# Decode step on one core: V caches issued from ScalarE's DMA queue instead of SyncE's

## The chip, the cores and the metric

The kernel runs on one core of one Trainium2 chip. Its time is the device time of one execution in microseconds (us); 121.77 us is the median of three runs before the change (121.72 to 121.81). A profile is one further execution, in which the hardware profiler records every instruction and every DMA packet. Its times are counted from the first instruction. In the views PE is TensorE (matmuls), PEld its weight loads, DVE VectorE, ACT ScalarE, POOL GpSimd; SPq and ACTq are the instructions with which SyncE and ScalarE issue DMA transfers. MiB below is 1,048,576 bytes; the profile's GB/s are in 10^9 bytes.

## The reference

One decode step for 8 sequences (one token each), model width 512. The input is normalised; one branch is attention over the last 1024 positions of a cached K and V (32 query heads, 8 key/value heads, head size 128), the other a gated feed-forward network (width 1792); the output is `x + attention * silu(ffn)`.

```python
xn = layernorm(x)                                  # x: 8 x 1 x 512
q  = (xn @ wq).reshape(8, 1, 32, 128)              # wq: 512 x 4096
k, v = k_cache[:, :, 3072:], v_cache[:, :, 3072:]  # 8 x 8 x 1024 x 128 each, 4 query heads share one
p  = softmax(q k^T / sqrt(128));  o = p v
s  = o.reshape(8, 1, 4096) @ wo                    # wo: 4096 x 512
f  = (gelu(xn @ w_gate) * (xn @ w_up)) @ w_down    # 512 x 1792, 512 x 1792, 1792 x 512
return x + s * silu(f)
```

Everything is bf16 in memory. What has to be read: K and V of a sequence 2 MiB each (8 sequences, together 32 MiB), wq 4 MiB, w_gate, w_up and w_down 1.75 MiB each, wo 4 MiB.

## The kernel before, in words

All large tensors go through one ring of 8 buffers of 2 MiB (`slot`). A buffer is given to the next tile as soon as the program's order says that its former tile is done with. A sequence's K or V (`load_cache`, L72) is two transfers of 1 MiB, `g` = 0 and 1, 128 rows of 8192 bytes each; called k3a and k3b below for sequence 3. wq is two transfers of 2 MiB (L93, rows of 16384 bytes); gate, up and down are one transfer each with rows of 14336 bytes (L422, L425); wo is three transfers of 1 MiB with rows of 8192 bytes and three last pieces of 640, 256 and 128 KiB (L436). All of these are issued by SyncE, in this order:

k0, wq, k1, v0, k2, v1, k3, v2, k4, v3, k5, v4, k6, v5, k7, v6, v7, gate, up, down, wo.

Only x (8 KiB) is issued by ScalarE, in one transfer. In the built program the completion of each transfer is counted on one of eight semaphores, taken by turns in the program's order, and a transfer is issued only when the transfer eight places before it in that order has landed. So at most eight transfers are under way, and each engine's queue issues in its own order: a transfer that must wait (for the eighth before it, or for its ring buffer) holds up those behind it on the same engine, and on ScalarE the arithmetic behind it too.

The work per sequence b, in the order of the loop at the kernel's middle: VectorE turns k(b+1)a (`turn_k`, L234), takes the row maximum of the scores of b (L305 to L312), turns k(b+1)b, and turns the probabilities (`turn_p`, L328). ScalarE makes the bias (L315), the exp (L317), and copies the result out of PSUM (`keep_o`, L352). TensorE does the scores of b+1 (L295) in two halves, the gathering of b-1's heads between them (L360, L364), and then the product with V (`values`, L339), whose second half of 32 matmuls reads the b half of V. The exp of b+1 stands behind `keep_o(b)` on ScalarE, and `keep_o(b)` needs `values(b)`, which needs V of b. `turn_k(b+1, 0)` stands ahead of the maximum of b on VectorE.

After the loop, strictly one behind the other: `gather(7)`, `regroup(1)` (L375 to L391), the gate and up products (L450), the gelu on ScalarE and VectorE (L460 to L473), the down product (L479), the product with wo (L498, `s_ps`, four groups of 32 matmuls), two VectorE operations (L506, L508) and the store. TensorE takes its instructions in that order, so the feed-forward products come after `values(7)` although they need nothing of it.

Of the kernel before, what the change touches and what calls it, by code (L numbers as in the profile page):

```python
# [21 lines left out]
def kernel(  # L22
# [13 lines left out]
    nc = tc.nc  # L36

    B, Sq, D = A_x.shape
# [23 lines left out]
    def slot(name):  # L62
        return ring.tile([P, 2 * ROW], BF16, name=name, tag="slot")


    x_sb = keep.tile([B, D], BF16, name="x_sb")
    nc.scalar.dma_start(out=x_sb, in_=A_x.flatten_outer_dims())

    def load_cache(cache, b, name):
        t = slot(name).rearrange("p (g x) -> p g x", g=NG)  # L70
        for g in range(NG):
            nc.sync.dma_start(  # L72
                out=t[:, g],
                in_=cache[b, g * HG : (g + 1) * HG, win0:Sk, :].rearrange(
                    "n (p c) d -> p n (c d)", c=C
                ),
            )
        return t

    k_sb, v_sb = {}, {}  # L80

    def load_k(b):
        k_sb[b] = load_cache(A_k_cache, b, "k_sb")

    def load_v(b):
        v_sb[b] = load_cache(A_v_cache, b, "v_sb")

    load_k(0)
    wq_v = A_wq.rearrange("(p k) n -> p k n", k=NK)
    wq_sb = []  # L90
    for i in range(2):
        t = slot("wq_sb").rearrange("p (k n) -> p k n", k=NK // 2)
        nc.sync.dma_start(out=t, in_=wq_v[:, i * (NK // 2) : (i + 1) * (NK // 2), :])  # L93
        wq_sb += [t[:, k, :] for k in range(NK // 2)]
    load_k(1)
    load_v(0)


# [3 lines left out]
        out=ident,  # L102
        in_=ident,
# [13 lines left out]
        out=xpad,  # L117
        in_=xpad,
# [17 lines left out]
        out=xhat,  # L136
# [9 lines left out]
    with tc.tile_pool(name="ps_x", bufs=1, space=PSUM) as ps_x:  # L146
# [26 lines left out]
        out=hv,  # L173
        in_=hv,
# [7 lines left out]
        out=neg_st,  # L182
        in_=neg_st,
# [8 lines left out]
        out=neg_mv,  # L192
        in_=neg_mv,
# [12 lines left out]
    for g in range(NG):  # L206
        nc.vector.tensor_reduce(
            out=sel[:, g, g * qd : (g + 1) * qd],
            in_=ident.rearrange("p (t g h) -> p g h t", t=4, g=NG)[:, g],
# [5 lines left out]
        out=own, in_=ident.rearrange("p (i e) -> p e i", e=8), axis=AX.X, op=ALU.add  # L215
    )
    pick = consts.tile([P, 4 * NU], BF16, name="pick")
    with nc.allow_low_precision(reason="sums of zeros and a single one"):
        nc.vector.tensor_reduce(
            out=pick, in_=ident.rearrange("p (a e) -> p a e", e=8), axis=AX.X, op=ALU.add  # L220
# [11 lines left out]
    def turn_k(b, g):  # L232
        t = kT_pool.tile([P, ROW], BF16, name="kT")
        nc.vector.transpose(out=t.bitcast(I32), in_=k_sb[b][:, g].bitcast(I32))  # L234
        kT[b, g] = t
# [7 lines left out]
    with tc.tile_pool(name="ps_q", bufs=1, space=PSUM) as ps_q:  # L243
# [10 lines left out]
        for half in range(2):  # L254
# [3 lines left out]
            for i in range(4 * half, 4 * half + 4, 2):  # L258
                sl = slice(i * 512, (i + 2) * 512)
                nc.vector.transpose(out=q_t[:, sl].bitcast(I32), in_=q_bf[:, sl].bitcast(I32))  # L260

    q_v = q_t.rearrange("p (g h m b r w) -> p m b r w g h", g=NG, h=qd, m=2, b=B, r=RB)
    for j in range(4):
        sl = slice(32 * j, 32 * j + 32)
# [15 lines left out]
    def scores(b, g):  # L280
        if g == 0:
            S[b] = ps_s.tile([P, 2, 512], FP32, name="S_ps")
            for half in range(2):
                nc.tensor.matmul(  # L284
                    S[b][:, half, :],
                    neg_st.rearrange("p j h -> p (j h)"),
                    neg_mv.rearrange("p a n -> p (a n)"),
                    start=True,
                    stop=False,
                )  # L290
        kv = kT[b, g].rearrange("p (c m i w) -> p c m i w", m=2, i=32, w=2)
        for m in range(2):
            for w in range(2):
                for half in range(2):
                    nc.tensor.matmul(  # L295
                        S[b][:, half, :],
                        qbd[:, m, b, w, g, :],
                        kv[:, half * 16 : (half + 1) * 16, m, :, w],
                        start=False,
                        stop=(g == NG - 1 and m == 1 and w == 1),  # L300
                    )

    def softmax(b):
        mx = two.tile([P, 1], FP32, name="mx")
        nc.vector.tensor_reduce(  # L305
            out=mx, in_=S[b].rearrange("p a c -> p (a c)"), axis=AX.X, op=ALU.max
        )

        m2 = two.tile([64, 1], FP32, name="m2")
        nc.vector.tensor_tensor(out=m2, in0=mx[0:64, :], in1=mx[64:128, :], op=ALU.max)  # L310
        m1 = two.tile([32, 1], FP32, name="m1")
        nc.vector.tensor_tensor(out=m1, in0=m2[0:32, :], in1=m2[32:64, :], op=ALU.max)  # L312
        nb = two.tile([P, 1], FP32, name="nb")
        for j in range(4):
            nc.scalar.mul(nb[32 * j : 32 * j + 32, :], m1, -inv)  # L315
        P_sb[b] = two.tile([P, C // 2, 32, 2], BF16, name="P_sb")
        nc.scalar.activation(  # L317
            out=P_sb[b].rearrange("p c i w -> p c w i"),
            in_=S[b].rearrange("p a (c w i) -> p (a c) w i", w=2, i=32),
            func=ACT.Exp,  # L320
            bias=nb,
            scale=inv,
            accum_out=sums[:, b : b + 1],
        )

    def turn_p(b):
        pT[b] = two.tile([P, C // 2, Hq, 2], BF16, name="pT")
        nc.vector.transpose(  # L328
            out=pT[b].rearrange("p c h w -> p (c h w)").bitcast(I32),
            in_=P_sb[b].rearrange("p c i w -> p (c i w)").bitcast(I32),  # L330
        )

    def values(b):
        O_ps[b] = ps_o.tile([P, NG, Dh], FP32, name="O_ps")
        for g in range(NG):
            vv = v_sb[b][:, g].rearrange("p (c d) -> p c d", d=Dh)
            for c in range(C):
                t = c % 4
                nc.tensor.matmul(  # L339
                    O_ps[b][32 * t : 32 * t + 32, g, :],  # L340
                    pT[b][:, c // 2, :, c % 2],
                    vv[:, c, :],
                    start=(c < 4),
                    stop=(c >= C - 4),
                )
# [4 lines left out]
    def keep_o(b):  # L350
        O_sb[b] = two.tile([P, NG, Dh], FP32, name="O_sb")
        nc.scalar.copy(out=O_sb[b], in_=O_ps[b])  # L352

    def gather(b):
        q = b % 4
        if q == 0:
            o_ps[b // 4] = ps_g.tile([P, Dh + 1], FP32, name="o_ps")
        o = o_ps[b // 4][32 * q : 32 * q + 32, :]
        for g in range(NG):
            nc.tensor.matmul(  # L360
                o[:, 0:Dh], sel[:, g, :], O_sb[b][:, g, :], start=(g == 0), stop=(g == NG - 1)
            )
        for g in range(NG):
            nc.tensor.matmul(  # L364
                o[:, Dh : Dh + 1],
                sel[:, g, :],
                sums[:, b : b + 1],
                start=(g == 0),
                stop=(g == NG - 1),
            )  # L370

    def regroup(q):

        rc = two.tile([P, 1], FP32, name="rc")
        nc.vector.reciprocal(out=rc, in_=o_ps[q][:, Dh : Dh + 1])  # L375
        o_x = two.tile([P, 8, Dh], BF16, name="o_x")
        nc.vector.scalar_tensor_tensor(
            out=o_x,
            in0=o_ps[q][:, 0:Dh].unsqueeze(1).broadcast_to([P, 8, Dh]),
            scalar=rc,  # L380
            in1=own.unsqueeze(2).broadcast_to([P, 8, Dh]),
            op0=ALU.mult,
            op1=ALU.mult,
        )
        ox_v = o_x.rearrange("p h (e j) -> p j (h e)", j=8)
        r_ps = ps_g.tile([P, 8, 4, NU], FP32, name="r_ps")
        for j in range(8):
            nc.tensor.matmul(
                r_ps[:, j], ox_v[:, j], pick, start=True, stop=True
            )  # L390
        nc.vector.tensor_copy(  # L391
            out=oT[:, :, :, 4 * RB * q : 4 * RB * (q + 1) : RB],
            in_=r_ps.rearrange("p j b u -> p j u b"),
        )
# [3 lines left out]
    for b in range(B):  # L398
        if b + 2 < B:
            load_k(b + 2)  # L400
        if b + 1 < B:
            load_v(b + 1)
            turn_k(b + 1, 0)
        softmax(b)
        if b + 1 < B:
            scores(b + 1, 0)
        if b >= 1:
            gather(b - 1)
        if b + 1 < B:
            turn_k(b + 1, 1)  # L410
            scores(b + 1, 1)
        turn_p(b)
        values(b)
        keep_o(b)
        if b == 4:
            regroup(0)
# [29 lines left out]
    for n, ws in (("z_ps", wgu[0]), ("u_ps", wgu[1])):  # L446
# [15 lines left out]
        out=z2, in0=z2, scalar1=0.044715, scalar2=1.0, op0=ALU.mult, op1=ALU.add  # L462
# [11 lines left out]
        out=hT.rearrange("p j b -> p (j b)"), in_=h_bf.rearrange("p (y j) -> p j y", j=NJ)  # L474
    )
    f_ps = ps_f.tile([P, DT], FP32, name="f_ps")
    for j in range(NJ):
# [11 lines left out]
        out=g_sb, in0=g_sb, scalar1=0.5, scalar2=0.5, op0=ALU.mult, op1=ALU.add  # L489
# [5 lines left out]
    for u in range(NU):  # L495
# [15 lines left out]
        out=out_f.rearrange("b (t d) -> t b d", t=4), in_=out_sb[0 : P : RB, :]  # L511
# [31 lines left out]
```

## Time and profile before

| what | before |
|---|---|
| median of three runs | 121.77 us |
| the profiled execution's own time | 121.8 us |
| its span, first to last instruction | 119.7 us |
| time outside the span | 2.1 us |
| busy: PE, DVE, ACT | 74.1, 75.8, 31.4 us |
| moved by DMA | 47.61 MB, mean 398 GB/s over the span |
| share of the SyncE queue's packets in 16 engines' span | 94.5% |
| granted TensorE clock, mean over the span | 0.837 |
| issue to landing of a K or V transfer, median | 19.9 and 19.6 us |

The profile page gives each engine's busy time, a strip of 40 slices with the busy share in tenths, the DMA queues by bytes, the chain of work that ended last, and groups of like instructions with their mean time and the idle time before them. The DMA share is the mean busy share of 16 DMA engines; near 1.0 none of them has an idle moment. Queue q1 carries SyncE's transfers, q10 ScalarE's, q8 and q14 fetch instructions.

### The profile page before, as it was taken

To read this page: it belongs to the slowest core of one execution; us is meant where nothing else is said; L and a number is where in the kernel's file an instruction comes from. 1 tells how busy PE (TensorE), PEld (TensorE's weight loads), DVE (VectorE), ACT (ScalarE), POOL (GpSimd) and SP (SyncE) were. 2 spreads that over 40 slices of the span, in tenths; PEclk is the share of its full clock that TensorE was granted. 3 is DMA by queue.
4 is the path that set the end of the run, shared out by engine and by line. 5 is a ranking of instruction groups with operands and counts; after the bars stand their busy time and mean duration, and the time that the engine had idled before them with its cause. 6 is when DMAs were issued, how large, how long until landed. Compare 5 with 4: busy or idle time off the path is not lost.

```text
span 119.7 us, 2300 instructions
## 1 busy us (share of the span) xinstructions
PE 74.1 (62%) x992; PEld 38.7 (32%) x992; DVE 75.8 (63%) x101; ACT 31.4 (26%) x75; POOL 3.2 (3%) x10
## 2 busy tenths in 40 slices
PE   0100499811994988969687684992994547535460
PEld 0100133300341544535443351450353433134340
DVE  3698820499739999999859959909943232651010
ACT  4600000676007151441612510700616110200000
POOL 2150000000000000000000000000000000000000
PEclk9999999985599999999999998599589755555555
DMA  2999999999999999999999999999999999999930
GB/s 66 394 457 433 411 416 427 430 433 422 427 427 433 419 419 427 435 411 430 430 433 405 430 430 430 411 430 435 424 419 447 422 451 412 434 403 430 402 118 3
DMA packets 6254, 47.61 MB, mean 398 GB/s; under 512 B 732, under 2 KB 868, under 8 KB 1124
## 3 DMA queue, kind: packets, MB, share of 16 engines
q1 hardware_dynamic: 6228, 47.46, 94.5%
q8 instruction: 8, 0.13, 0.4%
q10 hardware_dynamic: 16, 0.01, 0.0%
q14 instruction: 2, 0.02, 0.0%
HBM read 47.46 MB, written 0.01 MB: 397 GB/s over the span
## 4 chain that ended last, share of the span: by engine, by line
DMA 63%; PE 16%; DVE 14%; issue 2%; ACT 2%; SPq 1%; DVEq 0%
DMA wo_sb<-in_A_wo_dram 20%; DMA k_sb<-in_A_k_cache_dram 17%; DMA v_sb<-in_A_v_cache_dram 16%; DMA wq_sb<-in_A_wq_dram 9%; PE q_ps L247 8%; PE S_ps L295 6%; DVE kT L234 5%; DVE qbd L269 2%; DVE mx L305 2%; DVE q_both L260 1%; ACT P_sb L317 1%; PE s_ps L498 1%; DVE q_both L257 1%; SPq L72 1%; PE O_ps L339 1%
## 5 line engine op out<-in xcount | busy, mean ns | idle before, releaser
L295 PE MATMUL S_ps<-kT,qbd 128*128 128x512 bf16 x128 | 34.4, 416 | 14.9 <-DVE kT L234 11.5
L234 DVE STREAM_TRANSPOSE kT<-k_sb 128x2048 int32<-128x2048 int32 x16 | 36.5, 2289 | 4.6 <-DMA k_sb<-in_A_k_cache_dram 4.6
L295 PEld LDWEIGHTS <-qbd 128*128 128x128 bf16 x128 | 12.9, 103 | 32.4 <-issue 17.0
L247 PE MATMUL q_ps<-wq_sb,xnR 128*128 128x512 bf16 x32 | 9.8, 482 | 8.8 <-DMA wq_sb<-in_A_wq_dram 8.8
L315 ACT ACTIVATE nb<-m 32x1 f32<-32x1 f32 x32 | 6.4, 201 | 22.7 <-DVE m L312 22.4
L305 DVE TENSOR_REDUCE mx<-S_ps 128x1 f32<-128x1024 f32 x8 | 9.6, 1195 | 4.1 <-PE S_ps L295 4.1
L317 ACT ACTIVATE P_sb<-S_ps,nb 128x1024 bf16<-128x1024 f32 x8 | 11.1, 1391 | 0.3
L339 PE MATMUL O_ps<-v_sb,pT 128*32 128x128 bf16 x512 | 9.3, 228 | 2.6 <-DVE pT L328 2.6
L339 PEld LDWEIGHTS <-pT 128*32 128x32 bf16 x512 | 7.8, 101 | 5.6 <-issue 3.0
L352 ACT COPY O_sb<-O_ps 128x256 f32<-128x256 f32 x8 | 3.0, 372 | 23.5 <-PE O_ps L339 23.5
L247 PEld LDWEIGHTS <-xnR 128*128 128x128 bf16 x32 | 3.7, 118 | 14.6 <-issue 12.6
L328 DVE STREAM_TRANSPOSE pT<-P_sb 128x512 int32<-128x512 int32 x8 | 5.7, 711 | 3.4 <-ACT P_sb L317 2.8
L257 ACT CAST q_both<-q_ps 128x512 bf16<-128x512 f32 x6 | 3.0, 613 | 16.7 <-PE q_ps L247 16.7
L360 PE MATMUL o_ps<-O_sb,sel 128*32 128x128 f32 x32 | 6.1, 325 | 0.9 <-ACT O_sb L352 0.9
L498 PE MATMUL s_ps<-wo_sb,oT 128*32 128x128 bf16 x128 | 4.4, 307 | 3.4 <-DMA wo_sb<-in_A_wo_dram 3.3
L284 PE MATMUL S_ps<-neg_mv,neg_st 128*128 128x512 bf16 x16 | 4.8, 381 | 1.9 <-DVE q_both L257 1.9
L257 DVE CAST q_both<-q_ps 128x512 bf16<-128x512 f32 x2 | 1.3, 672 | 6.9 <-ACT q_both L257 6.9
L360 PEld LDWEIGHTS o_ps<-O_sb,sel 128*32 128x32 f32 x32 | 3.4, 128 | 5.0 <-issue 1.7
L498 PEld LDWEIGHTS <-oT 128*32 128x32 bf16 x128 | 3.5, 136 | 4.4 <-issue 4.2
L506 DVE TENSOR_TENSOR y<-s_ps,g_sb 128x128 f32<-128x128 f32 x1 | 0.3, 290 | 6.9 <-PE s_ps L498 6.9
L239 DVE MEMSET qbd<- 128x4096 uint32 x1 | 3.5, 3472 | 0.8 <-issue 0.8
L479 PE MATMUL f_ps<-wd_sb,hT 128*32 128x128 bf16 x56 | 1.7, 311 | 3.2 <-DVE hT L473 3.2
(64 smaller groups left out, 48.9 us busy)
## 6 DMA issues: line engine op xcount, KB each, us to landing
k_sb<-in_A_k_cache_dram SPq DMA_DIRECT2D x16, 1024.0 KB, 19.9
v_sb<-in_A_v_cache_dram SPq DMA_DIRECT2D x16, 1024.0 KB, 19.6
wq_sb<-in_A_wq_dram SPq DMA_DIRECT2D x2, 2048.0 KB, 11.3
wo_sb<-in_A_wo_dram SPq DMA_DIRECT2D x3, 1024.0 KB, 25.0
wgu_sb<-in_B_w_gate_dram SPq DMA_DIRECT2D x1, 1792.0 KB, 21.3
wgu_sb<-in_B_w_up_dram SPq DMA_DIRECT2D x1, 1792.0 KB
wd_sb<-in_B_w_down_dram SPq DMA_DIRECT2D x1, 1792.0 KB, 24.9
wo_sb<-in_A_wo_dram SPq DMA_DIRECT2D x1, 640.0 KB, 24.1
```

The lines of the kernel that those rows point to most:

```text
L234: nc.vector.transpose(out=t.bitcast(I32), in_=k_sb[b][:, g].bitcast(I32))
L247: nc.tensor.matmul(q_ps[i], xnR[:, k, :, :].rearrange("p j b -> p (j b)"), wq_sb[k][:, i * 512 : (i + 1) * 512], start=(k == 0), stop=(k = ...
L257: e(out=q_bf[:, i * 512 : (i + 1) * 512], in_=q_ps[i])
L284: nc.tensor.matmul(S[b][:, half, :], neg_st.rearrange("p j h -> p (j h)"), neg_mv.rearrange("p a n -> p (a n)"), start=True, stop=False,)
L295: nc.tensor.matmul(S[b][:, half, :], qbd[:, m, b, w, g, :], kv[:, half * 16 : (half + 1) * 16, m, :, w], start=False, stop=(g == NG - 1 an ...
L305: nc.vector.tensor_reduce(out=mx, in_=S[b].rearrange("p a c -> p (a c)"), axis=AX.X, op=ALU.max)
L315: nc.scalar.mul(nb[32 * j : 32 * j + 32, :], m1, -inv)
L317: nc.scalar.activation(out=P_sb[b].rearrange("p c i w -> p c w i"), in_=S[b].rearrange("p a (c w i) -> p (a c) w i", w=2, i=32), func=ACT.Exp,
L328: nc.vector.transpose(out=pT[b].rearrange("p c h w -> p (c h w)").bitcast(I32), in_=P_sb[b].rearrange("p c i w -> p (c i w)").bitcast(I32),)
L339: nc.tensor.matmul(O_ps[b][32 * t : 32 * t + 32, g, :], pT[b][:, c // 2, :, c % 2], vv[:, c, :], start=(c < 4), stop=(c >= C - 4),)
L360: nc.tensor.matmul(o[:, 0:Dh], sel[:, g, :], O_sb[b][:, g, :], start=(g == 0), stop=(g == NG - 1))
L498: nc.tensor.matmul(s_ps[32 * t : 32 * t + 32, :], oT[:, j, u, :], wo[u][:, j, t * DT : (t + 1) * DT], start=(u == 0 and j == 0), stop=(u = ...
```

## The change

K, wq and the weights stay with SyncE; V of sequence 0 too. V of sequences 1 to 7 is issued by ScalarE: v1 behind the casts of q (L257), v(b+2) behind the exp of b. In the old order v(b+1) was asked for at the top of iteration b; ScalarE's order is now exp(b), v(b+2)a, v(b+2)b, `keep_o(b)`. x comes in four transfers of two rows, all on ScalarE. The instructions of TensorE, VectorE and GpSimd are the same and stand in the same order.

The built program numbers the transfers of both engines in one order for the eight semaphores, so that a transfer of one engine can wait for one of the other: k3b waits until v1a has landed, v4a until v2a, wo's 640 KiB piece until v7a, the 128 KiB piece until v7b. The ring order is now v1, k2, v2, k3, v3, k4, v4, and so on to v7, then the weights; k5, k6 and k7 take the buffers of v0, v1 and v2 (they wait for `values` of 0, 1 and 2), gate that of v3, up that of k5, down that of v4, wo those of k6 and v5. SyncE's own order is k0, wq, k1, v0, k2, k3, k4, k5, k6, k7, gate, up, down, wo.

```diff
     x_sb = keep.tile([B, D], BF16, name="x_sb")
-    nc.scalar.dma_start(out=x_sb, in_=A_x.flatten_outer_dims())
-
-    def load_cache(cache, b, name):
+    for r in range(0, B, 2):
+        nc.scalar.dma_start(out=x_sb[r : r + 2], in_=A_x.flatten_outer_dims()[r : r + 2])
+
+    def load_cache(cache, b, name, queue):
         t = slot(name).rearrange("p (g x) -> p g x", g=NG)
         for g in range(NG):
-            nc.sync.dma_start(
+            queue.dma_start(
                 out=t[:, g],
...
     def load_k(b):
-        k_sb[b] = load_cache(A_k_cache, b, "k_sb")
+        k_sb[b] = load_cache(A_k_cache, b, "k_sb", nc.sync)
 
     def load_v(b):
-        v_sb[b] = load_cache(A_v_cache, b, "v_sb")
+        v_sb[b] = load_cache(A_v_cache, b, "v_sb", nc.sync if b == 0 else nc.scalar)
...
+    load_v(1)
     q_v = q_t.rearrange("p (g h m b r w) -> p m b r w g h", g=NG, h=qd, m=2, b=B, r=RB)
...
         if b + 2 < B:
             load_k(b + 2)
         if b + 1 < B:
-            load_v(b + 1)
             turn_k(b + 1, 0)
         softmax(b)
+        if b + 2 < B:
+            load_v(b + 2)
         if b + 1 < B:
             scores(b + 1, 0)
```

## The prediction

> **What bounds the kernel now.** I read the page first, then the chain of waits, then the stretches that the chain named.
>
> The page: the DMA strip is full from the second slice to the 38th, and one queue has nearly all of it.
>
> ```profile
> span 119.7 us, 2300 instructions
> DMA  2999999999999999999999999999999999999930
> q1 hardware_dynamic: 6228, 47.46, 94.5%
> ```
>
> The chain in order of time, its last part: 24 us of waiting for wo's transfers, then 2 us of arithmetic. What ends the kernel is the landing of the last bytes.
>
> ```profile
> 71.18 19.51 DMA v_sb<-in_A_v_cache_dram
> ...
> 90.71 24.12 DMA wo_sb<-in_A_wo_dram
> ...
> 114.87 1.30 PE s_ps L498 x32
> ```
>
> Stretches (columns: stretch, its length, busy time of PE, PEld, DVE, ACT, POOL, then granted clock, DMA share, GB/s): after 40.1 us the engines are never idle, at 426 GB/s. A 1 MiB transfer is 2.46 us of that.
>
> ```profile
> 0.00:40.10 40.10, 19.98 (x75) 7.75 (x76) 26.48 (x46) 11.30 (x22) 3.16 (x10) 0.91 0.96 398
> 40.10:93.20 53.10, 41.18 (x622) 22.00 (x620) 42.00 (x42) 18.21 (x49) 0.00 (x0) 0.94 1.01 426
> ```
>
> TensorE at the end, in order of time: the last `values`, then gather, regroup, gate, up, down, and wo's product, whose last three groups wait for wo.
>
> ```profile
> 94.08 1.71 PE L339 MATMUL O_ps<-v_sb,pT 128*32 128x128 bf16 x64 [2.56 <-DVE pT L328]
> 96.25 1.06 PE L360 MATMUL o_ps<-O_sb,sel 128*32 128x128 f32 x4 [0.47 <-ACT O_sb L352]
> ...
> 99.65 1.68 PE L450 MATMUL z_ps<-wgu_sb,xnR 128*32 128x448 bf16 x16
> ...
> 106.62 1.68 PE L479 MATMUL f_ps<-wd_sb,hT 128*32 128x128 bf16 x56 [3.19 <-DVE hT L473]
> 108.43 1.05 PE L498 MATMUL s_ps<-wo_sb,oT 128*32 128x128 bf16 x32
> ...
> 114.87 1.28 PE L498 MATMUL s_ps<-wo_sb,oT 128*32 128x128 bf16 x32 [0.46 <-DMA wo_sb<-in_A_wo_dram]
> ```
>
> SyncE's issues of wo: this one waits for v7b by its semaphore, so v7b landed at 93.16.
>
> ```profile
> 93.16 0.33 SPq L436 DMA_DIRECT2D wo_sb<-in_A_wo_dram  x1
> ```
>
> So today v7b is the last of K, V and wq (37.75 MB), and all 9.7 MB of weights land behind it. That is what hides the serial end. From the end of `values(7)` (95.79) to the start of `s_ps` (108.43) are 12.64 us; its 128 matmuls take 3.6 us back to back (56 of the same shape take 1.68 and 32 take 1.05, so 26 ns each more). It ends at 116.15. The second half of `values(7)`, 0.86 us, is what reads v7b. So v7b may land until 116.15 - 3.6 - 12.64 - 0.86 = 99.05 at no cost; after that every us is a us. The slack is 5.9 us, 2.5 MB.
>
> **The change part by part.** *x in four.* Three more issues on ScalarE at 0.58 us (x's own) put the normalisation back by 1.8 us: its last copy ends at 5.14, and TensorE's next work waits for wq until 13.60. VectorE's early work ends at 15.80, its next wait at 22.68. Cost 0; without that cover, 1.8 us.
>
> *SyncE's start.* k1b now waits for k0a, which landed at 6.2; k0b, wq and k1a (6 MiB, 15 us) lie ahead of it. v0 stands behind k1b, k2 waits for wq (13.5 and 18.4) with k1 and v0 ahead. The engines stay full: 0.
>
> *v1.* Issued behind the casts, at 25.0 instead of 13.5. k3b waits until v1a has landed and k4 until v1b has; about 5 MiB of v0, k2 and k3a are still queued at 25. Cost 0.
>
> *Two issues behind each exp.* They stand ahead of `keep_o(b)`, in a gap of 2.89 us on ScalarE that ends with `values(b)`; 2 x 0.58 = 1.16 us fit. v(b+2)a also waits there until v(b)a has landed, v(b+2)b until v(b)b, but `keep_o(b)` needs both anyway, and the issue runs beside `values(b)`. Queued behind are `keep_o(b)`, then the bias and exp of b+1. Cost 0; were the gap gone, 1.16 us in each of six iterations, on a chain that has slack to DMA from iteration 4 on.
>
> *SyncE loses 14 issues.* Its waits are for landings, not for issue time: 0.
>
> *V falls behind the weights.* This is the term that counts. Before, one queue fixed the order, v7 ahead of gate. Now gate, up, down and wo follow k7 on SyncE, and V competes with them. v2 can start only behind exp(0), which ends at 38.66; from issue to first bytes I take 1.44 us (SyncE's first issue at 0.81, engines working from about 2.25), so 40.1. By then q1 had moved 15.96 MB, which is the same in the new order, since nothing went idle. Of the 37.75 MB, 21.79 MB remain: v2 to v7, 12.58 MB, and K, 9.21 MB. V is not starved after that: with V(b) landed, V(b+1) is still whole, about 9.8 us at half rate, while `values`, `keep_o`, bias and exp (1.08 + 0.37 + 0.84 + 1.57 us) bring the next issue within 4 us.
>
> How two loaded queues share the engines, the trace does not show. That they share, it does: x was issued at 0.80 beside k0a at 0.81, and VectorE read x at 2.40, k0a landed at 6.2; and instruction packets arrive while q1 is full. The bounds are V served first and V served last (rivals below). Between them I take one packet each in turn, as the trace's unit of transport is a packet and a row of a tile is one (6254 packets, of which 1124 under 8 KB; K and V alone have 4096 rows). K and V rows are 8192 bytes, so they go even until K is done, and V then has 12.58 - 9.21 = 3.37 MB left, 411 rows. Against them stand gate, up and down with rows of 14336 bytes, 384 in all, 5.50 MB, and then 27 rows of wo, 0.22 MB. So 5.7 MB of weights go ahead of v7b, which lands 5.7 / 0.426 = 13.4 us later, at 106.6. Then 0.86 + 12.64 + 3.6 give 123.7 as the end of `s_ps` instead of 116.15: +7.5 us. TensorE's clock, 0.52 in the last stretch, is already low there, so I take the same durations.
>
> [...]
>
> The sum: 121.8 us (the profiled execution: span 119.7 and 2.1 outside) + 7.5 = 129.3. The median of the runs is 121.77, so nothing is to be corrected.
>
> **The rivals.** *Finer sharing, by bytes or by transfers* (0.24). Even in bytes, 3.37 MB of weights pass: 7.9 us, v7b at 101.1, `s_ps` ends at 118.2: 123.8. By whole transfers two of gate and up pass, 3.67 MB: 124.5; three, 5.5 MB: 128.8. For it: nothing shows that a row is the unit. Also, each stall of SyncE (k7 for `values(2)`, gate for `values(3)`) gives V the engines alone and shortens the loss.
>
> *V first* (0.04). Then k7b is the last of the 37.75 MB at 93.16: turn 2.29, scores 1.97, maximum 1.56, bias and exp 2.4, turn 0.71 put `values(7)` at 102.1 instead of 94.08, `s_ps` ends at 120.1: 125.7.
>
> *The mixed streams move less, or V comes last* (0.14). The one stretch with two loading queues, 2.0 to 4.5 us, moved 315 GB/s, though start-up is in it. 3% less from 27 to 107 us is 2.4 us: 131.7. At the bound v7b lands with the last wo piece, near 115.8: 115.8 + 17.1 = 132.9 for `s_ps`, 138.6. Against it: rows and totals are the same.
>
> *The change doesn't do what it says* (0.05). If both queues were drained in order of issue, v7, issued behind exp(5) (77.3), would meet at most gate ahead of it (issued at 76.2): 1.8 MB, under the slack of 2.5 MB, and the time stays 121.8.
>
> *Faster* (0.08). One mechanism: two queues keep the engines better fed. The best long stretch before, 4.5 to 13.5 us, moved 430 instead of 426 GB/s; over the 88 us from 27 on that is 0.8 us, 121.0. It decides only if v7b lands before 99.05, that is if fewer than 2.5 MB of weights pass V. The DMA share of 1.01 speaks against it. [...]
>
> **How the numbers follow.** Packets in turn 0.45, finer sharing 0.24, loss or V last 0.14, faster 0.08, no change 0.05, V first 0.04. 129.3 is the likeliest. The range 122.4 to 132.5 leaves out no change and faster (0.13) and half of the loss case (0.07). Within 0.2% (0.24 us) is about what a measurement of this kernel can't tell from no change: faster 0.08, same 0.05, slower 0.87.
>
> **What would show it.** In the new profile: two hardware queues, q1 near 32.8 MB and q10 near 14.7 MB; the DMA strip still full and the last wo piece landing near 115; `values(7)` waiting for V until about 106 with TensorE idle before it; `s_ps` back to back in some 3.6 us with no wait for wo; gate, up and down landed before v7b. Wrong would be: v7b before 99 (then the end stays with wo), a DMA strip with holes (then the rate is the cause), `keep_o` or exp late by the issues (then ScalarE is).

## The result and the profile after

The changed kernel takes 129.08 us (median of five runs, 128.84 to 130.06) against 121.76. The ratio on record, taken over the runs, is 1.0627, 95% interval 1.0603 to 1.0650; the two medians alone divide to 1.0601. The prediction was 129.3 us, range 122.4 to 132.5. The profiled execution is the slowest of the five (130.06 us, span 128.3); times read from its end stand about a microsecond above a typical run's.

The page of the changed kernel: span, DMA strip, and the two hardware queues with packets, MB and share.

```profile
span 128.3 us, 2304 instructions
...
DMA  3999999999999999999999999999999999960000
...
q1 hardware_dynamic: 4212, 32.78, 60.8%
q10 hardware_dynamic: 2032, 14.69, 27.2%
```

The strip is as full as before, but it ends four slices (some 13 us) ahead of the end: the loads are still done before 117, and the store is issued only at 125.71, instead of 116.84. Stretches of the changed kernel (length, busy time of PE, PEld, DVE, ACT, POOL, clock, DMA share, GB/s) say the same: two queues move 425 to 433 GB/s, one queue moved 426.

```profile
40.10:80.00 39.90, 29.15 (x440) 15.63 (x443) 32.55 (x32) 12.12 (x34) 0.00 (x0) 0.93 1.01 425
80.00:93.20 13.20, 9.75 (x139) 5.17 (x139) 9.49 (x11) 3.46 (x9) 0.00 (x0) 0.96 1.02 433
93.20:107.00 13.80, 3.31 (x72) 2.65 (x72) 0.71 (x1) 2.50 (x7) 0.00 (x0) 0.55 1.00 426
107.00:117.00 10.00, 6.04 (x80) 3.42 (x79) 2.90 (x5) 1.45 (x3) 0.00 (x0) 0.50 0.75 307
117.00:125.00 8.00, 5.08 (x184) 4.83 (x184) 3.13 (x6) 0.32 (x2) 0.00 (x0) 0.50 0.01 2
```

Where the time went stands in TensorE's rows of the end. The product with V of sequence 7 now stands in two halves, each waiting for its transfer; the second begins at 108.02. From there on every row waits for arithmetic alone, and the product with wo runs through in one piece.

```profile
96.18 1.04 PE L341 MATMUL O_ps<-v_sb,pT 128*32 128x128 bf16 x32 [6.04 <-DMA v_sb<-in_A_v_cache_dram]
...
102.93 1.04 PE L341 MATMUL O_ps<-v_sb,pT 128*32 128x128 bf16 x32 [4.00 <-DMA v_sb<-in_A_v_cache_dram]
108.02 1.04 PE L341 MATMUL O_ps<-v_sb,pT 128*32 128x128 bf16 x32 [4.04 <-DMA v_sb<-in_A_v_cache_dram]
109.53 1.06 PE L362 MATMUL o_ps<-O_sb,sel 128*32 128x128 f32 x4 [0.47 <-ACT O_sb L354]
...
112.94 1.68 PE L453 MATMUL z_ps<-wgu_sb,xnR 128*32 128x448 bf16 x16
...
119.92 1.69 PE L482 MATMUL f_ps<-wd_sb,hT 128*32 128x128 bf16 x56 [3.80 <-DVE hT L476]
121.38 3.63 PE L501 MATMUL s_ps<-wo_sb,oT 128*32 128x128 bf16 x128
```

How the queues share is read from the DMA view of two stretches of the changed kernel (queue: packets, MB, share of the stretch's time). From 48 to 80 us K runs beside V, rows of 8192 bytes on both sides:

```profile
q10 hardware_dynamic: 924, 6.78, 50.4%
q1 hardware_dynamic: 923, 6.74, 49.9%
```

From 84 to 103 us V runs beside weights, most of them in rows of 14336 bytes:

```profile
q1 hardware_dynamic: 408, 5.18, 63.7%
q10 hardware_dynamic: 405, 2.92, 36.6%
```

The number of packets is nearly the same on both queues in both stretches (about a tenth of them, 196 of 1851 and 90 of 814, are completion packets of 4 bytes); the bytes are not. V, which the serial end waits for, gets 36.6% of the engines beside the weights.

Equal counts would also come from longer turns of equal length, say eight rows each. The packet records of the trace settle that. They hold the queue, start and duration of every packet, though not the engine; but nearly every packet's end has a start 3 or 4 ns ahead of it (813 of 815 from 84 to 103 us), so successors can be matched by time. From 84 to 103 us 811 of 813 packets are followed by one of the other queue, from 48 to 80 us 1834 of 1848; a completion packet takes a turn like a row. In the kernel before, which has one loading queue, it is 8 of 2614 from 45 to 90 us, all of them beside instruction fetches.

### The profile page after: what moved, and what is told of

Same layout as the page of the kernel before. It is cut to its first block, busy times and chain, and to the rows that moved or that the text cites. A ratio compares the mean times of both kernels' runs of the same rounds, so it can differ in the third digit from the quotient of the medians.

```text
span 128.3 us, 2304 instructions
## 1 busy us (share of the span) xinstructions
PE 73.1 (57%) x985; PEld 39.4 (31%) x992; DVE 75.5 (59%) x101; ACT 31.2 (24%) x75; POOL 3.2 (2%) x10
## 4 chain that ended last, share of the span: by engine, by line
DMA 58%; PE 19%; DVE 13%; ACT 2%; issue 2%; ACTq 1%; SPq 1%; DVEq 0%
DMA v_sb<-in_A_v_cache_dram 49%; DMA wq_sb<-in_A_wq_dram 9%; PE q_ps L248 7%; PE S_ps L297 4%; PE s_ps L501 3%; DVE qbd L271 2%; DVE mx L307 2%; DVE kT L235 2%; ACTq L73 1%; PE f_ps L482 1%; PE z_ps L453 1%; DVE q_both L261 1%; ACT nb L317 1%; DVE o_x L379 1%; DVE q_both L258 1%
## 5 line engine op out<-in xcount | busy, mean ns | idle before, releaser
L297 PE MATMUL S_ps<-kT,qbd 128*128 128x512 bf16 x128 | 33.6, 409 | 11.3 <-DVE kT L235 7.6
L341 PE MATMUL O_ps<-v_sb,pT 128*32 128x128 bf16 x512 | 10.6, 237 | 19.1 <-DMA v_sb<-in_A_v_cache_dram 19.0
L341 PEld LDWEIGHTS <-pT 128*32 128x32 bf16 x512 | 8.5, 104 | 22.8 <-issue 22.8
L286 PE MATMUL S_ps<-neg_mv,neg_st 128*128 128x512 bf16 x9 | 3.5, 407 | 1.9 <-DVE q_both L258 1.9
L393 DVE CAST oT<-r_ps 128x128 bf16<-128x128 f32 x2 | 0.9, 430 | 6.1 <-PE r_ps L390 6.1
L129 DVE BATCH_NORM_STATS2 stats<-x_sb 8x6 f32<-8x512 bf16 x1 | 0.7, 683 | 5.8 <-DMA x_sb<-in_A_x_dram 5.8
```

The costliest lines, as they stand in the source:

```text
L297: nc.tensor.matmul(S[b][:, half, :], qbd[:, m, b, w, g, :], kv[:, half * 16 : (half + 1) * 16, m, :, w], start=False, stop=(g == NG - 1 an ...
L341: nc.tensor.matmul(O_ps[b][32 * t : 32 * t + 32, g, :], pT[b][:, c // 2, :, c % 2], vv[:, c, :], start=(c < 4), stop=(c >= C - 4),)
```

## The experiments

The theory: V falls behind the weights because the queues take turns packet by packet, and the serial work behind the last V then hangs over the end of the loads. Rivals: two queues move less; the issues and waits on ScalarE hold up the iterations; x in four takes part; the queues share by bytes or by whole transfers. Times are medians; ratios are those on record, to the kernel before on the same chip, with their 95% intervals.

### One part alone: x in four transfers

```diff
 # on the kernel before
-    nc.scalar.dma_start(out=x_sb, in_=A_x.flatten_outer_dims())
+    for r in range(0, B, 2):
+        nc.scalar.dma_start(out=x_sb[r : r + 2], in_=A_x.flatten_outer_dims()[r : r + 2])
```

> The kernel before with one part of the change alone: x in four transfers, V still on SyncE. Theory 1 (the loss is V falling behind the weights, packet by packet): no part of it is x's, so 121.8 us, within 0.3. Rival (the late normalisation, first bias at 8.0 us instead of 3.3 in the changed kernel, is part of the loss): 122.5 or more.

Measured: 121.51 us, ratio 0.9984 (0.9974 to 0.9994). x has no part in the loss.

### The change without x in four

```diff
 # on the changed kernel
-    for r in range(0, B, 2):
-        nc.scalar.dma_start(out=x_sb[r : r + 2], in_=A_x.flatten_outer_dims()[r : r + 2])
+    nc.scalar.dma_start(out=x_sb, in_=A_x.flatten_outer_dims())
```

> The changed kernel with x in one transfer again; V as in the changed kernel. Theory 1: the whole loss is V's: 128.8 to 130. Rival (x in four takes part in it): below 128.5.

Measured: 128.88 us, ratio 1.0590 (1.0573 to 1.0606). The loss is V's.

### V of the last sequence back on SyncE

```diff
 # on the changed kernel
-        v_sb[b] = load_cache(A_v_cache, b, "v_sb", nc.sync if b == 0 else nc.scalar)
+        v_sb[b] = load_cache(A_v_cache, b, "v_sb", nc.sync if b in (0, B - 1) else nc.scalar)
```

> The changed kernel, but V of sequence 7 is issued by SyncE behind k7 and so ahead of gate; v1 to v6 stay with ScalarE, x in four. Theory 1: no weight can pass v7b any more, it lands near 93 to 96 us, inside the slack that ends at 99, and the time is 121.8 (up to 122.5). Rival (two queues move less, or the issues on ScalarE delay the iterations): six sequences of V still go that way, so at least three quarters of the 7.3 us stay, 127 or more.

Measured: 121.23 us, ratio 0.9963 (0.9952 to 0.9973). Two of fourteen transfers moved back take away the whole loss, with twelve still on ScalarE; the time is 0.6 us below the 121.8 that was expected (the end of this document comes back to that). TensorE's rows of this run:

```profile
96.39 1.90 PE L341 MATMUL O_ps<-v_sb,pT 128*32 128x128 bf16 x64 [1.71 <-DVE pT L330]
...
113.34 0.63 PE L501 MATMUL s_ps<-wo_sb,oT 128*32 128x128 bf16 x32 [0.90 <-DMA wo_sb<-in_A_wo_dram]
114.85 0.46 PE L501 MATMUL s_ps<-wo_sb,oT 128*32 128x128 bf16 x20 [0.88 <-DMA wo_sb<-in_A_wo_dram]
115.51 0.61 PE L501 MATMUL s_ps<-wo_sb,oT 128*32 128x128 bf16 x12 [0.20 <-DMA wo_sb<-in_A_wo_dram]
```

The product with V of sequence 7 waits for the probabilities and not for V, and the product with wo waits for wo, as in the kernel before. A cost of the two queues as such, or of the issues on ScalarE, would still be there.

### The feed-forward products ahead of the last V

```diff
 # on the changed kernel; the blocks are moved, their tiles take score and output buffers of PSUM
         turn_p(b)
+        if b == B - 1:
+            ...   # issue of the weights, gate and up products, gelu, turning h
         values(b)
 ...
     gather(B - 1)
+    ...           # down product
     regroup(1)
```

> The changed kernel with the gate and up products and the gelu put ahead of the product with V of sequence 7, and the down product between the last gather and the last regroup; the queues are as in the changed kernel. Theory 1: v7b lands as late as in the changed kernel (107 to 108), but behind it are only half of the product with V (1.0), copy 0.4, gather 1.3, down 1.7, regroup 1.2, the product with wo 3.6: it ends near 117 instead of 125, and the time is 121.5 to 122.9. Rival (the end is set by the rate of the queues, so by the last weights): no change, 129.

Measured: 121.27 us, ratio 0.9973 (0.9957 to 0.9988), 0.2 us below the range that was expected. The chain of waits of this run ends so:

```profile
81.38 25.10 DMA v_sb<-in_A_v_cache_dram
...
106.50 9.27 DMA wo_sb<-in_A_wo_dram
...
115.80 0.27 PE s_ps L503 x4
```

v7b is as late as the change makes it (106.48), and it costs nothing: with less serial work behind it, the end is the landing of wo again. So it is not the late landing by itself but the 17 us of work in order behind it.

### Weights in shorter rows, transfers cut in two

```diff
 # on the changed kernel; down likewise, in two halves of 7 rows
-        nc.sync.dma_start(out=tv, in_=w.rearrange("(p k) f -> p k f", k=NK))
+        wv = w.rearrange("(p k) f -> p k f", k=NK)
+        for k0 in range(0, NK, 2):
+            nc.sync.dma_start(out=tv[:, k0 : k0 + 2, :], in_=wv[:, k0 : k0 + 2, :])
```

> The changed kernel with gate, up and down loaded in rows of 7168 bytes instead of 14336 (two transfers each of half the size), the same bytes on the same queue in the same order. Theory 1, with one packet each in turn: V then gets 8192 of every 15360 bytes instead of 8192 of 22528; the last four transfers of V take 4.6 us each instead of 6 to 6.7, v7b lands 6 to 7 us earlier, near 101, and the time is 122.4 to 123.9. Rival (the queues share by bytes, or by whole transfers with some other cause of the loss): by bytes nothing changes, 129.1; by whole transfers also about half, 124 to 126.

Measured: 122.86 us, ratio 1.0080 (1.0054 to 1.0106). Same bytes, same queues, same order, and six of the seven microseconds are gone; the second half of the last product with V begins at 100.74. Sharing by bytes would have left 129.1. Whole transfers in turn I had put at 124 to 126; but halved transfers also halve what passes V in one turn, so this run alone does not rule that out. The next does.

### Weights in shorter rows, the transfers left whole

```diff
 # on the changed kernel; down likewise, and the products read the pieces where they now lie
-        tv = slot("wgu_sb")[:, 0 : NK * F].rearrange("p (k f) -> p k f", k=NK)
-        nc.sync.dma_start(out=tv, in_=w.rearrange("(p k) f -> p k f", k=NK))
+        tv = slot("wgu_sb").rearrange("p (h x) -> p h x", h=2)[:, :, 0 : NK * F // 2]
+        nc.sync.dma_start(out=tv, in_=w.rearrange("(p h k) f -> p h (k f)", h=2, k=NK // 2))
```

> The changed kernel with gate, up and down still one transfer each of the same size, but laid into their buffers in two pieces a partition with a gap between, so that a row is 7168 bytes instead of 14336. Number, size and order of the transfers are those of the changed kernel. One row each in turn: a V transfer beside them takes 4.6 us instead of 6.75, v7b lands near 101 and the time is that of the run with the transfers cut in two (122.86), 122.4 to 123.4. One whole transfer each in turn: nothing changes, 129.1.

Measured: 123.17 us, ratio 1.0099 (1.0072 to 1.0126). The turn is a row, not a transfer: with twice as many rows in a transfer of the weights, whole transfers in turn would have given them nearly twice V's packets. The DMA view of this run, 88 to 95 us:

```profile
q10 hardware_dynamic: 213, 1.52, 52.0%
q1 hardware_dynamic: 218, 1.45, 49.2%
```

Again the packets are nearly equal in number, and V has the larger half of the bytes because its rows are now the longer ones. On TensorE the two halves of the last product with V are 4.7 us apart; 128 rows of each queue, 128 x (8192 + 7168) bytes = 1.97 MB, at the 425 GB/s of 88 to 95 us are 4.6.

```profile
96.53 1.04 PE L341 MATMUL O_ps<-v_sb,pT 128*32 128x128 bf16 x32 [1.99 <-DMA v_sb<-in_A_v_cache_dram]
101.26 1.05 PE L341 MATMUL O_ps<-v_sb,pT 128*32 128x128 bf16 x32 [3.68 <-DMA v_sb<-in_A_v_cache_dram]
```

### Shorter still

The same edit with gate and up in four pieces a partition (3584 bytes) and down in seven (2048 bytes).

> As the run before, with gate and up in rows of 3584 bytes and down in rows of 2048, again one transfer each. One row each in turn: V gets 8192 of every 11776 bytes or more, its transfers take 3.6 us or less, v7b lands near 96 to 97, inside the slack that ends at 99, and the loss is gone: 121.3 to 122.2. If something other than V's landing holds the end, or rows this small slow the queues down, more than 122.5.

Measured: 121.63 us, ratio 0.9994 (0.9984 to 1.0004): no different from the kernel before. 88 to 95 us in the DMA view, then TensorE's rows:

```profile
q10 hardware_dynamic: 279, 2.05, 69.2%
q1 hardware_dynamic: 271, 0.97, 33.9%
```

```profile
97.37 1.05 PE L341 MATMUL O_ps<-v_sb,pT 128*32 128x128 bf16 x32 [2.34 <-DMA v_sb<-in_A_v_cache_dram]
...
115.37 1.23 PE L503 MATMUL s_ps<-wo_sb,oT 128*32 128x128 bf16 x32 [0.66 <-DMA wo_sb<-in_A_wo_dram]
```

v7b is there by 97.4, inside the slack that was worked out to end at 99.05, and the last product waits for wo again. Three layouts of the weights in whole transfers give three landings in the profiled executions (108.0, 101.3, 97.4) and three median times (129.1, 123.2, 121.6).

### Both cures together

V of sequence 7 on SyncE and the feed-forward products ahead of it.

> The two changes that took the loss away, together: V of sequence 7 on SyncE ahead of gate, and the gate and up products ahead of the product with V of sequence 7. Theory 1: each alone leaves the end to the last bytes of wo, so together they bring nothing more than the better of them: 121.0 to 121.5. If the 0.4 us that each was below the kernel before came from slack in TensorE's end, they add up: 120.6 to 120.9.

Measured: 121.17 us, ratio 0.9956 (0.9941 to 0.9972), with V of sequence 7 alone 121.23. They do not add up; both only give the end back to wo. It is, with 121.23, the fastest that was run, below the kernel before by about 0.4%.

## Why the prediction was right, point by point

**What bounds the kernel, and the slack.** Right. The step from the landing of v7b to the end of the product with wo was put at 0.86 + 12.64 + 3.6 = 17.1 us; measured 125.01 - 108.02 = 17.0, and 16.5 in the run with x in one transfer (107.15 to 123.65). The slack up to 99.05 is borne out by a landing at 97.4, after which the last product still waited for wo, and by one at 101.3, 2.2 us past it: there the product ran through without waiting for wo, and the store was issued 2.1 us later than in the kernel before (118.96 against 116.84).

**V behind the weights, 5.7 MB in 13.4 us.** Right in kind and a little too small. v7b was put at 106.6; it came at 108.0 in the profiled execution and at 107.15 in the run with x in one transfer, whose profiled execution is a typical one. K, wq and v0 are 23.07 MB of SyncE's queue; by v7b's landing that queue had moved 30.12 MB (in brackets, here and below, the run with x in one transfer: 29.78), so 7.1 MB of weights (6.7). In the kernel before, SyncE's queue had moved 38.50 MB by 93.16, 0.75 MB of it weights. So 6.3 MB more (6.0) went ahead instead of 5.7, and at 426 GB/s 14.8 us (14.0), as the landings show.

Two of the step's own terms were off. V of sequence 2 was taken to start at 40.1, 1.44 us behind the end of exp(0); ScalarE issued it while exp(0) still ran, at 37.60, but its first row moved only at 41.38. So when K's last row started, at 83.4, V had 3.66 MB left and not 3.37. And I had taken 1:1 in packets between two bounds without a row that told it; the packet records above and the runs with shorter rows now show it. Nor did x beside k0a show that two queues share at all, as the prediction read it: x's last packet was over at 2.1 us, and k0a's first began at 2.25.

That the time itself came within 0.2 us is partly luck: the five runs spread over 1.2 us, and in the run with x in one transfer the later landing (107.15 for 106.6) and the shorter serial work (16.5 for 17.1 us) cancel to the 123.7 that was worked out for the end of `s_ps`.

**SyncE's stalls.** The prediction, under its first rival, let them shorten the loss, since V would have the engines alone. SyncE did wait, up to 14.4 us for a V transfer of ScalarE's before it issued down at 89.44, but its queue had work all the while: from 10 to 107 us no two of its packets start more than 0.22 us apart.

**ScalarE's issues at no cost.** Right: the gap from exp to `keep_o` is 2.89 us in iterations 0 to 2 as before (later it is V that is waited for), and the kernel with twelve V transfers on ScalarE is not slower (121.23 us).

**SyncE's start and v1 at no cost.** Right: the stretch up to 40.1 us moves 398 GB/s in both kernels. v1 was issued at 23.53, not 25.0, and its first row moved at 27.55.

**x in four, 1.8 us of delay, covered.** Covered, but mis-sized: VectorE waits 5.8 us for x instead of 1.1, and the normalisation is 4.7 us late (rows of ScalarE, before and after):

```profile
3.32 0.29 ACT L132 ACTIVATE rstd<-mv,eps_sb 8x1 f32<-8x1 f32 x1 [0.62 <-DVE mv L130]
```

```profile
8.02 0.29 ACT L133 ACTIVATE rstd<-mv,eps_sb 8x1 f32<-8x1 f32 x1 [4.36 <-DVE mv L131]
```

TensorE still waits 4.3 us for wq afterwards, so nothing came of it.

**The rivals.** Finer sharing by bytes fell with the run in halved transfers, whole transfers in turn with the run that left them whole. V first (125.7 us) and queues drained in order of issue (121.8) fell with V's 36.6% of the engines beside the weights and the 129.08. Fewer bytes moved fell by the stretches: 425 to 433 GB/s with two loaded queues, 426 with one. A gain of the mixed queues of 0.8 us did not show there either. The measured turn is one row, or one completion packet: 811 of 813 packets from 84 to 103 us have one of the other queue behind them.

## What to carry to other kernels

When loads bound a kernel, the order of the bytes is part of the design: in these runs one queue kept it (0.75 MB of weights had moved when v7b landed), two queues gave it up to turns of one row each (7.1 MB in the changed kernel), and the queue with the longer rows got more (there from 84 to 103 us 63.7% of the engines against 36.6%, most rows 14336 bytes against 8192). Before moving loads to a second queue, look for what is wanted last but has serial work behind it, work out its slack from the row that waits last at the end, and count how many bytes of the other queue will pass it. The cure can be as small as moving the last such load back, or taking independent work out from behind it.

## What the runs showed of the hardware that I had not expected

- ScalarE's first rows came late on engines that were already full (SyncE's queue at 102.2% from 23 to 27.4 us): v1 was issued at 23.53 and its first row moved at 27.55, v2 at 37.60 and 41.38, so 4.0 and 3.8 us. SyncE's first transfer, on empty engines, was issued at 0.81 and its first row moved at 2.25, so 1.44 us. What makes the difference was not tried.
- x in four transfers was there 4.7 us later than in one, not the 1.8 us of three more issues. The packets of the one transfer moved between 1.75 and 2.1 us, before k0a's first row at 2.25; of the four, the last three moved between 3.7 and 6.6 us, beside SyncE's rows.
- In the changed kernel ScalarE issued v2, which stands behind exp(0) in the program, while exp(0) still ran: exp(0) from 37.54 for 1.39 us, the issue of v2 at 37.60.
- With V of sequence 7 on SyncE, with the feed-forward products first, and with both, the kernel was 0.3 to 0.4% below the kernel before. Up to the issue of the store they are alike (116.84 before, 116.82 and 116.74 in two of them); from there to the end of the execution the kernel before takes 4.96 us and they take 4.34. That is one profiled execution each, the kernel with the shortest rows has the same 4.33 behind a store at 117.30, and x in four alone has 4.60. What makes the difference was not tried.
